# Splitting 64-bit weights: three vector passes a piece replaced by one rounding add into the low 16 bits

## The chip, the cores and the metric

The kernel runs on one core of one Trainium2 chip. The metric is the device time of one execution, in microseconds. Before the change the median of three runs is 871.97 us (870.41, 871.97 and 872.31).

## What is computed

A linear attention with a decaying state, then two blocks of dense layers. The activations are float32. The weights of both blocks are float64, since the setup divides them by a float64 square root. Cut to what matters:

```
state = 0                                   # per batch and head, 48 x 48
for t in range(768):
    y[t]  = r[t] @ (state + (u * k[t]) outer v[t])
    state = w * state + k[t] outer v[t]
x = y as 3072 tokens x 384
h = max(x @ w1, x @ w2, x @ w3)             # 384 -> 768, weights float64
x = h @ w_out                               # 768 -> 384
g, val = x @ w_gate, x @ w_val              # 384 -> 1536
out = (silu(g) * val) @ w_out2              # 1536 -> 384, float32
```

## The kernel before

**Products.** Every product of the dense layers runs on TensorE (PE) as three matmuls in the type float32r: high part of the weight by high part of the input (L429), high by low (L430), low by high (L431). So each weight is needed as two float32r tiles, its high and its low part. The tokens go in six blocks of 512 (index i). In the first block of layers a step f (of 6) makes three products `m` with 128 output channels each from the tile `w_a` of that step; the products `o` then use `w_b`; the second block of layers has products `g` and `oo` with `w_c`. The attention runs in 24 units n (six blocks of time, four batches): `s` (scores), `y` and `u` on PE. Unit n belongs to token block n // 4, so the units of block i + 1 are worked on between the products of block i.

**Pieces of weights.** A weight tile comes from DRAM in pieces k of 576 columns (384 for `w_b`), 42 in all: 12 for `w_a`, 6 for `w_b`, 24 for `w_c`. Pieces 0 to 14 are wanted while the first token block is worked on. A piece of 128 x 576 float64 lands as pairs of 32-bit words in the tile `raw` (three buffers); `lw` is the low and `hw` the high word, each read with a step of 8 bytes. `t` (two buffers) takes the float32 that is made of it. The steps of one piece in the kernel before:

- `fetch` (L212): the DMA from DRAM, in SP's queue.
- `scale` (L224), ScalarE (ACT): `hw`, read as float32, times 2^-112 into `t`.
- `top` (L257, L259), VectorE (DVE): shift and mask, then the sign put back: `t` is the weight cut off to a short mantissa.
- `rest` (L265, L267), DVE: the bits that were cut off, gathered from both words into `lw`.
- `power` (L272), DVE: the exponent bits of `t` into `hw`.
- `put_hi` (L275), ACT: `t` to the high part. `to_float` (L279), ACT: the integer in `lw` to float32.
- `put_lo` (L283), POOL: `hw` times `lw` to the low part.

**Order.** The order of the steps on each engine is not that of the code. `Plan.run` (L107) goes through a list of steps with needs and assumed costs and puts the step that can start first, weighted by the work behind it, next on its engine; engines then run their rows in that order. PE's order is written out by hand (L626 to L648). The steps of the pieces are added in L682 to L706; the numbers there (TOP, REST, POWER) are the planner's costs in us. A `fetch` of piece k needs `lo` of piece k - 3 (its buffer of `raw`), `scale` needs `hi` and `power` of piece k - 2 (its buffer of `t`). SP's queue is in order: a DMA whose buffer isn't free holds all behind it.

**The branch.** Some 33 us into the program all engines pass a branch (L615) that chooses between two forms of the recurrence. `fetch` of pieces 3 and on stands behind it, pieces 0 to 2 are loaded at the start. After it the first token block is split into a high part (`xhi`, L420, ACT) and a low part (`xlo`, L424, POOL: input less high part), as is every later one. For token block 1 and on, `repack` (L409, DMA) and `choose` (L415, DVE) come ahead of that.

Of the kernel before, what the change touches and what calls it, by code (L numbers as in the profile page):

```python
# [8 lines left out]
F32 = mybir.dt.float32  # L9
F32R = mybir.dt.float32r  # L10
U8 = mybir.dt.uint8
U32 = mybir.dt.uint32
I32 = mybir.dt.int32
AF = mybir.ActivationFunctionType
ALU = mybir.AluOpType
# [11 lines left out]
HALF = 576  # L27
# [60 lines left out]
class Plan:  # L88
# [8 lines left out]

    SHARED = ("top", "rest", "power", "lo", "xlo", "ylo", "scaled", "bonus", "choose")

# [73 lines left out]
def rwkv_moe(ctx: ExitStack, tc: tile.TileContext, qk, nat, kn, vn, rn, wcol, wh, uh, wup1, wout1, wup2, out):  # L173
# [80 lines left out]
    def top(k):  # L254

        t, hw = ts[k], words(k)[1]
        nc.vector.tensor_scalar(out=t, in0=t, scalar1=3, scalar2=0xFFFFF000,  # L257
                                op0=ALU.logical_shift_left, op1=ALU.bitwise_and)
        nc.vector.scalar_tensor_tensor(out=t, in0=hw, scalar=0x80000000, in1=t,  # L259
                                       op0=ALU.bitwise_and, op1=ALU.bitwise_or)  # L260

    def rest(k):

        lw, hw = words(k)
        nc.vector.tensor_scalar(out=hw, in0=hw, scalar1=0x1FF, scalar2=15,  # L265
                                op0=ALU.bitwise_and, op1=ALU.logical_shift_left)
        nc.vector.scalar_tensor_tensor(out=lw, in0=lw, scalar=17, in1=hw,  # L267
                                       op0=ALU.logical_shift_right, op1=ALU.bitwise_or)

    def power(k):  # L270

        nc.vector.tensor_scalar(out=words(k)[1], in0=ts[k], scalar1=0xFF800000, scalar2=None, op0=ALU.bitwise_and)  # L272

    def put_hi(k):
        nc.scalar.copy(part(k, 0), ts[k].bitcast(F32))  # L275

    def to_float(k):
        lw = words(k)[0]
        nc.scalar.mul(lw.bitcast(F32), lw, 2.0**-35)  # L279

    def put_lo(k, eng):
        lw, hw = (x.bitcast(F32) for x in words(k))
        eng.tensor_tensor(out=part(k, 1), in0=hw, in1=lw, op=ALU.mult)  # L283
        del raws[k], ts[k]

# [220 lines left out]
    with tc.manual_schedule():  # L506
# [175 lines left out]
        for k, (key, z, n, _) in enumerate(jobs):  # L682
            early = key[0] == "c" and key[1] < ASIDE
            own, pace, space = {}, [], []
            TOP, REST, POWER, share = (1.22, 1.22, 0.46, n / HALF) if key[0] != "c" else (1.22, 1.22, 0.46, 1.0) if early else (1.25, 1.25, 0.46, 1.0)
            if early:
# [4 lines left out]
            if k < 3:  # L691
                add(("fetch", k), {"none": 0.0}, [], lambda e: None, at=17.5 + 1.7 * k)
            else:
                add(("fetch", k), {"sync": 0.5}, [("lo", k - 3), ("branch",)] + pace, lambda e, k=k: fetch(k), lag=3.5, **own)
            cast = {"act": 0.2 + 0.48 * share}
            add(("scale", k), cast, [("fetch", k)] + ([("hi", k - 2), ("power", k - 2)] if k > 1 else []), lambda e, k=k: scale(k), **own)
            add(("top", k), {"dve": TOP * share}, [("scale", k)] + ([("power", k - 1)] if k else []), lambda e, k=k: top(k), **own)
            add(("rest", k), {"dve": REST * share}, [("top", k)], lambda e, k=k: rest(k), **own)
            add(("power", k), {"dve": POWER * share}, [("rest", k)], lambda e, k=k: power(k), **own)
            add(("hi", k), cast, [("top", k), ("rest", k)] + space + ([("put", k - 1)] if early and k > nearly else []),  # L700
                lambda e, k=k: put_hi(k), **own)
            add(("float", k), cast, [("rest", k)], lambda e, k=k: to_float(k), **own)
            add(("lo", k), {"pool": 1.2 * share, "dve": 0.76 * share}, [("float", k), ("power", k), ("hi", k)],
                lambda e, k=k: put_lo(k, engine[e]), **own)
# [210 lines left out]
```

## Time and profile before

| | |
|---|---|
| runs | 870.41, 871.97, 872.31 us; median 871.97 us |
| profiled execution | span 868.4 us from the first to the last instruction; its device time is not shown beside it |
| busy, whole span | PE 849.5 us (98%), DVE 404.0 (47%), ACT 317.6 (37%), POOL 195.6 (23%) |
| mean granted clock of PE | 0.994 of full speed |
| DMA | 74.33 MB, 86 GB/s over the span |

The span is 3.6 us under the median of the runs. A share of busy time is a mean over the whole span. The stages differ much: the span's 40 slices show DVE at nine tenths in slices 3 to 5 (44 to 109 us) and at two tenths in the second half, while PE stands at nine tenths from there to the end. A row of a group of instructions gives its line, engine, operation, tiles (written <- read), shape, count, then busy us and mean ns of one, then the idle time of the engine just ahead of them and what ended it. The prediction goes by the rows in the section below.

### The profile page before, as it was taken

The numbers are of one execution on the slowest core, as the hardware profiler recorded it, in microseconds if no ns is written. First come the engines' busy times: TensorE is split into PE (matmuls) and PEld (weight loads), VectorE is DVE, ScalarE is ACT, GpSimd is POOL, SyncE is SP. The second block draws the span as 40 slices with busy tenths as digits, with TensorE's granted clock in tenths as the row PEclk, the third lists the DMA queues.
The fourth block names the chain that finished last, engine by engine and source line by source line (L and its number), as shares of the span: only waits on it lengthen the run. The fifth ranks groups of instructions, "written<-read, shape, count | busy, mean of one in ns | idle before, by whom it ended". The sixth has DMA issues, their size and how long they took to land.

```text
span 868.4 us, 11958 instructions
## 1 busy us (share of the span) xinstructions
PE 849.5 (98%) x4794; PEld 697.5 (80%) x4794; DVE 404.0 (47%) x629; ACT 317.6 (37%) x634; POOL 195.6 (23%) x188
## 2 busy tenths in 40 slices
PE   9889799999999999999999999999999999999998
PEld 8667588888888888888888888888888888888886
DVE  4799977646746745313578422222222212122221
ACT  5666565344354443222455321131132122113111
POOL 7645453433523512100223300010010010001000
PEclk9899999999999999999999999999999999999999
DMA  8566424536346424421043100010000000001001
GB/s 286 194 204 204 162 85 121 164 126 196 137 138 188 159 84 160 173 105 59 11 127 109 37 1 1 0 37 1 1 37 1 1 1 36 1 1 37 0 1 37
DMA packets 21722, 74.33 MB, mean 86 GB/s; under 512 B 2496, under 2 KB 3392, under 8 KB 20896
## 3 DMA queue, kind: packets, MB, share of 16 engines
q1 hardware_dynamic: 21664, 73.54, 25.5%
q8 instruction: 38, 0.62, 0.3%
q14 instruction: 20, 0.16, 0.1%
HBM read 58.39 MB, written 14.16 MB: 84 GB/s over the span
## 4 chain that ended last, share of the span: by engine, by line
PE 87%; DVE 6%; issue 2%; ACT 0%; POOL 0%; ACTq 0%; DVEq 0%
PE g L429 11%; PE g L430 11%; PE g L431 11%; PE m L429 8%; PE m L430 7%; PE m L431 7%; PE oo L429 6%; PE oo L430 6%; PE oo L431 6%; PE o L431 3%; PE o L430 3%; PE o L429 3%; PE s L342 2%; PE y L371 2%; PE y L362 2%
## 5 line engine op out<-in xcount | busy, mean ns | idle before, releaser
L430 PE MATMUL g<-xlo,w_c 128*128 128x512 f32 x432 | 168.2, 389 | 0.0
L431 PE MATMUL g<-xhi,w_c 128*128 128x512 f32 x432 | 168.2, 389 | 0.0
L429 PE MATMUL g<-xhi,w_c 128*128 128x512 f32 x432 | 168.2, 389 | 0.0
L486 DVE TENSOR_TENSOR g<-mm,g 128x512 f32<-128x512 f32 x72 | 50.1, 696 | 243.5 <-PE g L431 243.4
L429 PE MATMUL m<-xhi,w_a 128*128 128x512 f32 x324 | 129.7, 400 | 1.6 <-ACT h L443 1.2
L431 PE MATMUL m<-xhi,w_a 128*128 128x512 f32 x324 | 127.0, 392 | 2.9 <-POOL w_a L283 2.9
L430 PE MATMUL m<-xlo,w_a 128*128 128x512 f32 x324 | 127.1, 392 | 1.6 <-POOL xlo L424 1.6
L482 ACT ACTIVATE mm<-g 128x512 f32<-128x512 f32 x72 | 43.0, 597 | 154.6 <-PE g L431 154.6
L424 POOL TENSOR_TENSOR xlo<-x,xhi 128x512 fp32r<-128x512 f32 x18 | 23.5, 1333 | 329.8 <-ACT xhi L420 329.8
L431 PEld LDWEIGHTS g<-xhi,w_c 128*128 128x128 f32 x432 | 81.1, 188 | 16.9
L429 PEld LDWEIGHTS g<-xhi,w_c 128*128 128x128 f32 x432 | 81.1, 188 | 16.8
L430 PEld LDWEIGHTS g<-xlo,w_c 128*128 128x128 f32 x432 | 81.1, 188 | 16.7
L491 ACT CAST gs<-g 128x512 fp32r<-128x512 f32 x72 | 42.2, 587 | 134.7 <-DVE g L486 134.7
L430 PE MATMUL oo<-gs,w_c 128*128 128x512 f32 x216 | 84.1, 389 | 0.0
L431 PE MATMUL oo<-gs,w_c 128*128 128x512 f32 x216 | 84.1, 389 | 0.0
L429 PE MATMUL oo<-gs,w_c 128*128 128x512 f32 x216 | 84.1, 389 | 0.0
L431 PEld LDWEIGHTS m<-xhi,w_a 128*128 128x128 f32 x324 | 60.9, 188 | 17.9 <-POOL w_a L283 5.2
L429 PEld LDWEIGHTS m<-xhi,w_a 128*128 128x128 f32 x324 | 60.8, 188 | 17.3 <-ACT h L443 1.5
L430 PEld LDWEIGHTS m<-xlo,w_a 128*128 128x128 f32 x324 | 60.9, 188 | 14.7 <-POOL xlo L424 3.0
L463 DVE TENSOR_TENSOR gs<-g,gs 128x512 fp32r<-128x512 f32 x72 | 49.8, 691 | 44.9 <-ACT gs L491 44.9
L333 ACT ACTIVATE am<-aeye,a 128x128 f32<-128x128 f32 x192 | 59.7, 392 | 23.2 <-DVE a L325 23.2
L460 ACT CAST hs<-m 128x512 fp32r<-128x512 f32 x33 | 19.3, 586 | 101.9 <-DVE m L448 101.4
(111 smaller groups left out, 1180.8 us busy)
## 6 DMA issues: line engine op xcount, KB each, us to landing
raw<-in_wup SPq DMA_DIRECT2D x36, 576.0 KB, 5.1
nat<-in_nat SPq DMA_DIRECT2D x22, 576.0 KB, 5.2
qk<-in_qk SPq DMA_DIRECT2D x24, 448.0 KB, 4.5
aside<-parts SPq DMA_DIRECT2D x12, 576.0 KB, 3.6
w_c<-aside SPq DMA_DIRECT2D x6, 1152.0 KB, 5.6
out<-ob SPq DMA_DIRECT2D x18, 256.0 KB, 2.1
y<-x SPq DMA_DIRECT2D x3, 768.0 KB, 10.7
raw<-in_wout SPq DMA_DIRECT2D x6, 384.0 KB, 3.3
```

The lines of the kernel that those rows point to most:

```text
L333: eng.mul(o, aeye, f)
L342: nc.tensor.matmul(sc[n][x][:, j], a[r:r + D, 1, j], a[r:r + D, 0, j], start=True, stop=True)
L362: nc.tensor.matmul(y[r:r + m, j], st[b][r:r + D, j * D:j * D + m], a[r:r + D, 0, j], start=j == 0, stop=False, skip_group_check=True)
L424: eng.tensor_tensor(out=lo[:, k], in0=t[:, k], in1=hi[:, k].bitcast(F32), op=ALU.subtract)
L429: nc.tensor.matmul(p, wh_, xh, start=first, stop=False)
L430: nc.tensor.matmul(p, wh_, xl, start=False, stop=False)
L431: nc.tensor.matmul(p, wl_, xh, start=False, stop=last)
L460: nc.scalar.copy(hsplit[i, f][0], banks["m", i, f, 2])
L463: nc.vector.tensor_tensor(out=g[1], in0=p, in1=g[0].bitcast(F32), op=ALU.subtract)
L482: nc.scalar.activation(out=hs[i, f], in_=banks["g", i, f, 0], func=AF.Silu)
L486: nc.vector.tensor_tensor(out=p, in0=hs[i, f], in1=p, op=ALU.mult)
L491: nc.scalar.copy(t[:, 0], banks["g", i, f, 1])
```

## The change

`top` keeps all bits that a float32 has room for: L257 loses its mask. `rest` becomes one pass (line 265 of the changed kernel): it views the low 16 bits of each word of `t` as uint16 and adds to them the low word of the weight times 2^-29, rounded by the write. So `t` is then the weight rounded to float32, and `raw` is free. `power` and `to_float` are gone. `put_hi` now comes behind `rest`; its cast to float32r rounds. `put_lo`, still on POOL, takes the high part off `t`. The needs follow: `fetch` of piece k waits for `rest` of k - 3 instead of `lo`, `scale` for `lo` of k - 2, since `t` is now read until the end. The planner's costs of `top` and `rest` change too.

```diff
     def top(k):
         t, hw = ts[k], words(k)[1]
-        nc.vector.tensor_scalar(out=t, in0=t, scalar1=3, scalar2=0xFFFFF000,
-                                op0=ALU.logical_shift_left, op1=ALU.bitwise_and)
+        nc.vector.tensor_scalar(out=t, in0=t, scalar1=3, scalar2=None, op0=ALU.logical_shift_left)
         nc.vector.scalar_tensor_tensor(out=t, in0=hw, scalar=0x80000000, in1=t,
                                        op0=ALU.bitwise_and, op1=ALU.bitwise_or)
     def rest(k):
-        lw, hw = words(k)
-        nc.vector.tensor_scalar(out=hw, in0=hw, scalar1=0x1FF, scalar2=15,
-                                op0=ALU.bitwise_and, op1=ALU.logical_shift_left)
-        nc.vector.scalar_tensor_tensor(out=lw, in0=lw, scalar=17, in1=hw,
-                                       op0=ALU.logical_shift_right, op1=ALU.bitwise_or)
-    def power(k):
-        nc.vector.tensor_scalar(out=words(k)[1], in0=ts[k], scalar1=0xFF800000, scalar2=None, op0=ALU.bitwise_and)
+        low = ts[k].bitcast(U16).rearrange("p (n z) -> p n z", z=2)[:, :, 0]
+        nc.vector.scalar_tensor_tensor(out=low, in0=words(k)[0], scalar=2.0**-29, in1=low,
+                                       op0=ALU.mult, op1=ALU.add)
+        del raws[k]
-    def to_float(k):
-        lw = words(k)[0]
-        nc.scalar.mul(lw.bitcast(F32), lw, 2.0**-35)
     def put_lo(k, eng):
-        lw, hw = (x.bitcast(F32) for x in words(k))
-        eng.tensor_tensor(out=part(k, 1), in0=hw, in1=lw, op=ALU.mult)
-        del raws[k], ts[k]
+        eng.tensor_tensor(out=part(k, 1), in0=ts[k].bitcast(F32), in1=part(k, 0).bitcast(F32), op=ALU.subtract)
+        del ts[k]
...
-            TOP, REST, POWER, share = (1.22, 1.22, 0.46, n / HALF) if key[0] != "c" else (1.22, 1.22, 0.46, 1.0) if early else (1.25, 1.25, 0.46, 1.0)
+            TOP, REST, share = (1.22, 0.76, n / HALF) if key[0] != "c" else (1.25, 0.8, 1.0)
...
-                add(("fetch", k), {"sync": 0.5}, [("lo", k - 3), ("branch",)] + pace, lambda e, k=k: fetch(k), lag=3.5, **own)
+                add(("fetch", k), {"sync": 0.5}, [("rest", k - 3), ("branch",)] + pace, lambda e, k=k: fetch(k), lag=3.5, **own)
-            add(("scale", k), cast, [("fetch", k)] + ([("hi", k - 2), ("power", k - 2)] if k > 1 else []), lambda e, k=k: scale(k), **own)
-            add(("top", k), {"dve": TOP * share}, [("scale", k)] + ([("power", k - 1)] if k else []), lambda e, k=k: top(k), **own)
+            add(("scale", k), cast, [("fetch", k)] + ([("lo", k - 2)] if k > 1 else []), lambda e, k=k: scale(k), **own)
+            add(("top", k), {"dve": TOP * share}, [("scale", k)] + ([("rest", k - 1)] if k else []), lambda e, k=k: top(k), **own)
-            add(("lo", k), {"pool": 1.2 * share, "dve": 0.76 * share}, [("float", k), ("power", k), ("hi", k)],
+            add(("lo", k), {"pool": 1.2 * share, "dve": 0.76 * share}, [("hi", k)],
```

PE has the same rows in the same order in both programs, tile for tile. The other engines' orders move, since the planner sees other costs and needs. In the rows below a number in a tile's name is the piece (`t_2`), the unit (`qk_4`) or the block and step (`m_0_1_2`); the last number only tells buffers apart.

VectorE from the branch on, before (in the change the lines behind `put_lo` are numbered 10 lower: L301 there is L311 here, L438 is L448):

```order
L265 TENSOR_SCALAR raw_1_131<-raw_1_131 128x576
L267 SCALAR_TENSOR_TENSOR raw_1_131<-raw_1_131 128x576
L272 TENSOR_SCALAR raw_1_131<-t_1_400 128x576
L257 TENSOR_SCALAR t_2_624<-t_2_624 128x576
L259 SCALAR_TENSOR_TENSOR t_2_624<-raw_2_133,t_2_624 128x576
L265 TENSOR_SCALAR raw_2_133<-raw_2_133 128x576
L267 SCALAR_TENSOR_TENSOR raw_2_133<-raw_2_133 128x576
L272 TENSOR_SCALAR raw_2_133<-t_2_624 128x576
L257 TENSOR_SCALAR t_3_642<-t_3_642 128x576
L259 SCALAR_TENSOR_TENSOR t_3_642<-raw_3_617,t_3_642 128x576
```

The same place on VectorE in the change:

```order
L258 TENSOR_SCALAR t_2_622<-t_2_622 128x576
L259 SCALAR_TENSOR_TENSOR t_2_622<-raw_2_133,t_2_622 128x576
L265 SCALAR_TENSOR_TENSOR t_2_622<-raw_2_133,t_2_622 128x576
L258 TENSOR_SCALAR t_3_639<-t_3_639 128x576
L259 SCALAR_TENSOR_TENSOR t_3_639<-raw_3_612,t_3_639 128x576
L438 TENSOR_TENSOR h_0_0_650<-h_0_0_650,m_0_0_1_667 128x512
L265 SCALAR_TENSOR_TENSOR t_3_639<-raw_3_612,t_3_639 128x576
L258 TENSOR_SCALAR t_4_700<-t_4_700 128x576
L259 SCALAR_TENSOR_TENSOR t_4_700<-raw_4_616,t_4_700 128x576
L301 TENSOR_TENSOR qk_4_662<-qk_4_662,powers_624 112x512 x2
```

Piece 1 is now done on VectorE ahead of the branch, and `top` of piece 4 stands ahead of the two passes on `qk_4`, which the first scores behind the branch (`s` of unit 4) wait for; before it stood behind them.

SP's queue from the branch on, before:

```order
L215 DMA raw_3_617<-in_wup1 128x1152
L304 DMA qk_4_665<-in_qk 112x1024
L305 DMA nat_4_666<-in_nat 128x1152
L215 DMA raw_4_683<-in_wup1 128x1152
L304 DMA qk_5_691<-in_qk 112x1024
```

The same place in SP's queue in the change:

```order
L216 DMA raw_3_612<-in_wup1 128x1152
L216 DMA raw_4_616<-in_wup1 128x1152
L294 DMA qk_4_662<-in_qk 112x1024
L295 DMA nat_4_663<-in_nat 128x1152
L216 DMA raw_5_683<-in_wup1 128x1152
```

Piece 4 moved ahead of the loads of unit 4.

VectorE at the end of the first token block (`choose` is L415, in the change L405), before:

```order
L257 TENSOR_SCALAR t_14_1269<-t_14_1269 128x384
L259 SCALAR_TENSOR_TENSOR t_14_1269<-raw_14_1227,t_14_1269 128x384
L265 TENSOR_SCALAR raw_14_1227<-raw_14_1227 128x384
L267 SCALAR_TENSOR_TENSOR raw_14_1227<-raw_14_1227 128x384
L272 TENSOR_SCALAR raw_14_1227<-t_14_1269 128x384
L404 TENSOR_TENSOR st_3_140<-st_3_140,u_7_1243 112x192
L448 TENSOR_TENSOR h_0_5_1229<-h_0_5_1229,m_0_5_1_1255 128x512
L448 TENSOR_TENSOR m_0_5_2_1276<-h_0_5_1229,m_0_5_2_1276 128x512
L311 TENSOR_TENSOR qk_8_1133<-qk_8_1133,powers_627 112x512
L415 COPY_PREDICATED xr_1_885<-slow_162,x2_1_89 128x1536
```

The same place on VectorE in the change:

```order
L258 TENSOR_SCALAR t_14_1233<-t_14_1233 128x384
L259 SCALAR_TENSOR_TENSOR t_14_1233<-raw_14_1168,t_14_1233 128x384
L265 SCALAR_TENSOR_TENSOR t_14_1233<-raw_14_1168,t_14_1233 128x384
L438 TENSOR_TENSOR h_0_5_1195<-h_0_5_1195,m_0_5_1_1210 128x512
L438 TENSOR_TENSOR m_0_5_2_1235<-h_0_5_1195,m_0_5_2_1235 128x512
L301 TENSOR_TENSOR qk_8_1120<-qk_8_1120,powers_624 112x512
L405 COPY_PREDICATED xr_1_872<-slow_162,x2_1_89 128x1536
```

`choose` of block 1 keeps its place behind piece 14, the last two maxima of block 0 and half of `qk_8`; two passes of piece 14 ahead of it are gone.

## Rows read from the trace of the kernel before

**Rows 1.** The page: the chain that ended last, shares of the span by engine.

```profile
PE 87%; DVE 6%; issue 2%; ACT 0%; POOL 0%; ACTq 0%; DVEq 0%
```

**Rows 2.** Stages: from:to, length, busy (count) of PE PEld DVE ACT POOL, clock, DMA, GB/s.

```profile
0.00:34.40 34.40, 30.84 (x274) 26.77 (x274) 19.09 (x46) 19.35 (x46) 24.13 (x35) 0.90 0.76 253
34.40:106.00 71.60, 60.54 (x493) 45.56 (x491) 68.58 (x108) 45.07 (x95) 36.63 (x34) 1.00 0.58 185
106.00:112.20 6.20, 6.20 (x20) 4.97 (x21) 5.62 (x8) 3.83 (x9) 6.09 (x5) 0.72 0.40 142
112.20:500.00 387.80, 387.80 (x2406) 319.00 (x2405) 223.98 (x344) 166.77 (x345) 113.60 (x105) 1.00 0.37 122
500.00:863.80 363.80, 363.80 (x1607) 301.24 (x1605) 86.43 (x125) 81.97 (x140) 15.13 (x12) 1.00 0.03 9
```

**Rows 3.** PE's waits from 34.4 to 106: total us, times, longest.

```profile
PE m L431 <- POOL w_a L283: 2.9, 4, 1.2
PE o L431 <- POOL w_b L283: 2.8, 2, 1.4
PE m L430 <- POOL xlo L424: 1.6, 3, 0.8
PE s L342 <- DVE qk L311: 1.6, 1, 1.6
PE m L429 <- ACT h L443: 1.2, 1, 1.2
PE u L390 <- DVE st L404: 0.6, 1, 0.6
PE m L429 <- ACT w_a L275: 0.3, 1, 0.3
```

**Rows 4.** Groups on VectorE from 34.4 to 106, shapes apart.

```profile
L267 DVE SCALAR_TENSOR_TENSOR raw<-raw 128x576 uint32<-128x576 uint32 x11 | 11.1, 1013 | 0.4
...
L265 DVE TENSOR_SCALAR raw<-raw 128x576 uint32<-128x576 uint32 x10 | 7.0, 705 | 0.1
L272 DVE TENSOR_SCALAR raw<-t 128x576 uint32<-128x576 uint32 x11 | 6.1, 558 | 0.3
...
L265 DVE TENSOR_SCALAR raw<-raw 128x384 uint32<-128x384 uint32 x3 | 1.7, 569 | 0.2
...
L272 DVE TENSOR_SCALAR raw<-t 128x384 uint32<-128x384 uint32 x3 | 1.1, 359 | 0.1
```

**Rows 5.** The timeline of VectorE from 37 us: start, us, instruction.

```profile
37.24 1.49 DVE L257 TENSOR_SCALAR t<-t 128x576 uint32<-128x576 uint32 x1 [1.22 <-ACT t L224]
38.77 1.58 DVE L259 SCALAR_TENSOR_TENSOR t<-raw,t 128x576 uint32<-128x576 uint32 x1
...
40.89 0.76 DVE L267 SCALAR_TENSOR_TENSOR raw<-raw 128x576 uint32<-128x576 uint32 x1
...
42.06 0.46 DVE L257 TENSOR_SCALAR t<-t 128x576 uint32<-128x576 uint32 x1
```

**Rows 6.** The timeline of POOL: while VectorE did the above, and two passes much later.

```profile
35.66 2.75 POOL L424 TENSOR_TENSOR xlo<-xr,xhi 128x512 fp32r<-128x512 f32 x2
...
484.49 1.15 POOL L283 TENSOR_TENSOR w_c<-raw 128x576 fp32r<-128x576 f32 x1 [3.70 <-ACT raw L279]
491.56 3.79 POOL L424 TENSOR_TENSOR xlo<-x,xhi 128x512 fp32r<-128x512 f32 x3 [5.92 <-ACT xhi L420]
```

**Rows 7.** The waits of the pieces from 34 to 112 (all engines; SP's queue).

```profile
ACT t L224 <- DMA raw<-in_wup: 9.2, 3, 5.1
...
SPq L215 <- POOL w_a L283: 36.2, 10, 7.2
```

**Rows 8.** The timeline of SP and ACT: the fetch of piece 4 and its `scale`.

```profile
40.28 0.39 SPq L215 DMA_DIRECT2D raw<-in_wup  x1
...
47.53 0.73 ACT L224 ACTIVATE t<-raw 128x576 f32<-128x576 f32 x1 [5.09 <-DMA raw<-in_wup]
```

**Rows 9.** The stage ahead of the low clock, columns as in rows 2.

```profile
88.00:106.00 18.00, 12.49 (x87) 8.60 (x85) 17.31 (x30) 10.02 (x21) 7.86 (x9) 1.00 0.40 131
```

More of the change, by code (lines that the diff above doesn't have):

```diff
@@ L11 @@
 U8 = mybir.dt.uint8
+U16 = mybir.dt.uint16
 U32 = mybir.dt.uint32
@@ L95, in __init__ @@
         self.behind = {}
-    SHARED = ("top", "rest", "power", "lo", "xlo", "ylo", "scaled", "bonus", "choose")
+    SHARED = ("top", "rest", "lo", "xlo", "ylo", "scaled", "bonus", "choose")
     def add(self, key, on, needs, do, lag=0.0, at=0.0, behind=None):
@@ L693, in rwkv_moe @@
             else:
-                add(("fetch", k), {"sync": 0.5}, [("lo", k - 3), ("branch",)] + pace, lambda e, k=k: fetch(k), lag=3.5, **own)
+                add(("fetch", k), {"sync": 0.5}, [("rest", k - 3), ("branch",)] + pace, lambda e, k=k: fetch(k), lag=3.5, **own)
             cast = {"act": 0.2 + 0.48 * share}
-            add(("scale", k), cast, [("fetch", k)] + ([("hi", k - 2), ("power", k - 2)] if k > 1 else []), lambda e, k=k: scale(k), **own)
-            add(("top", k), {"dve": TOP * share}, [("scale", k)] + ([("power", k - 1)] if k else []), lambda e, k=k: top(k), **own)
+            add(("scale", k), cast, [("fetch", k)] + ([("lo", k - 2)] if k > 1 else []), lambda e, k=k: scale(k), **own)
+            add(("top", k), {"dve": TOP * share}, [("scale", k)] + ([("rest", k - 1)] if k else []), lambda e, k=k: top(k), **own)
             add(("rest", k), {"dve": REST * share}, [("top", k)], lambda e, k=k: rest(k), **own)
-            add(("power", k), {"dve": POWER * share}, [("rest", k)], lambda e, k=k: power(k), **own)
-            add(("hi", k), cast, [("top", k), ("rest", k)] + space + ([("put", k - 1)] if early and k > nearly else []),
+            add(("hi", k), cast, [("rest", k)] + space + ([("put", k - 1)] if early and k > nearly else []),
                 lambda e, k=k: put_hi(k), **own)
-            add(("float", k), cast, [("rest", k)], lambda e, k=k: to_float(k), **own)
-            add(("lo", k), {"pool": 1.2 * share, "dve": 0.76 * share}, [("float", k), ("power", k), ("hi", k)],
+            add(("lo", k), {"pool": 1.2 * share, "dve": 0.76 * share}, [("hi", k)],
                 lambda e, k=k: put_lo(k, engine[e]), **own)
```

## The prediction

> **What bounds the kernel now.** The chain that ended last is 87% PE and 6% DVE [rows 1]. Such a share is a mean, so I cut the span into stages [rows 2]: the reader is to look for a stage in which PE isn't busy throughout. From 112.2 to 863.8 us PE is busy for 387.80 of 387.80 and 363.80 of 363.80 us: there nothing that another engine saves can shorten anything. Ahead of 34.4 us TensorE waits for the attention's first units, and only pieces 0 and 1 are worked on. One stage is left: from 34.4 to 106 PE is busy for 60.54 of 71.60 us, so it stands still for 11.1 us, while DVE is busy for 68.58 us, 96%. So in this stage VectorE is the bound, and it's the stage in which pieces 2 to 14 have to be there in time. Behind it, from 106.0 to 112.2, the granted clock is 0.72, a mixture of 2.4 and 1.2 GHz, after a stretch (88 to 106 us) in which PE was busy for only 12.49 of 18 us [rows 9]. That costs 6.20 x 0.28 = 1.7 us more. What the change can reach at most is thus 11.1 + 1.7 = 12.8 us of 868.4.
>
> Next, what PE waits for there [rows 3]. Three kinds, told apart by who is late:
> - weights: 2.9 and 2.8 us for the low part (POOL L283), 0.3 for the high part: 6.0 us;
> - VectorE's queue: 1.6 for `qk` of unit 4, 1.2 for a copy on ACT that stands behind a maximum on DVE, 0.6 for the state: 3.4 us;
> - the first `xlo` behind the branch: 1.6 us.
>
> **The change, part by part.** VectorE first. Per piece L265 and L272 go. In the stage that is 7.0 + 6.1 us for the wide pieces and 1.7 + 1.1 for the narrow ones, 15.9 us [rows 4]. All groups on VectorE in this stage add up to 74.5 us where the engine is busy for 68.58, since neighbouring rows overlap a little; so the removed ones are worth 15.9 x 68.58 / 74.5 = 14.6 us of its time. L257 loses only its mask: a pass with one operand over 576 words takes 0.46 us alone [rows 5], and the same with one operation instead of two; nothing. The new L265 takes the place of L267, with the same number of elements and two sources. No row shows a pass that writes 16-bit words with a step of 4 bytes and mixes types. Nearest is L267 itself, 0.76 us alone [rows 5] and 1.01 in the stage [rows 4]; a gain below that is excluded, since two sources at 576 elements never ran faster here; the other end is taken as twice, 1.5 us. I take 0.76. So VectorE's load falls from 68.6 to 54.0 us, where PE's own work is 60.5: the bound goes to PE, with VectorE close behind, at nine tenths.
>
> ACT loses `to_float` (L279), 42 passes. ACT is busy for 45.07 of 71.60 us [rows 2], so its load counts for nothing; what counts is that a piece goes through one pass less before POOL.
>
> POOL: `put_lo` now reads two tiles, `t` and the high part, instead of two halves of one. Alone it took 1.15 us for 576 elements, while the like subtraction `xlo` takes 3.79 / 3 = 1.26 us for 512 [rows 6], which makes 1.42 for 576. I take 1.42, bounds 1.15 and 1.5: 0.27 more a piece. POOL is busy for 36.63 of 71.60 us, so this is covered unless VectorE has to wait for it (a rival below).
>
> The fetches: the longest of SP's waits in this stage is the one of `fetch` for `put_lo` of the piece three earlier, 36.2 us in ten waits [rows 7]; it now waits for `rest`, two steps earlier. Piece 4 gains most: before, its DMA stood behind the load of unit 4, was issued at 40.28, and ACT waited for it for 5.09 us until 47.53 [rows 8]; now it is issued right behind piece 3, with which the queue goes on after the branch at some 33 us: 7 us earlier. The loads of unit 4 that it's moved past come later by one issue, 0.4 us [rows 8], and on VectorE `qk_4` stands behind three pieces in any case. In turn `scale` waits for `put_lo` of the piece two earlier: with two buffers of `t` a piece may take two times 5 us from `scale` to the end (a step of PE, some 10 us, uses two pieces), and needs about 0.73 + 0.46 + 0.76 + 0.76 + 0.73 + 1.42 = 4.9 without waits (the high part's cast on ACT taken like `scale` [rows 8]). It fits, and I cost it at nothing; should VectorE lag, it is the first thing to be late.
>
> What is late next: the split of token block 1. PE goes from the last `y` of block 0 through `u`, two products `m` (18 matmuls) and 27 of `o` without a gap, some 11 us; `repack`, `choose` and the split need nearly as long, and before were hidden behind late weights. I count 0.5 us of new waits there.
>
> The sum. Weight waits 6.0 to 1.0: -5.0. VectorE's queue 3.4 to 1.4, since it stays at nine tenths: -2.0. `xlo` stays. New wait: +0.5. The low clock: with PE busy for more than nine tenths of the stretch ahead of it, as it is behind 112 us where the clock is 1.00, I take -1.4 of 1.7. Sum: -7.9 us. The span would be 868.4 - 7.9 = 860.5. The profiled execution's span stands 3.6 us under the median of the runs; with that the time is **864.1 us**.
>
> **The rivals.**
>
> *All of it.* VectorE is no bound at all, and every wait for weights and for its queue goes with the low clock: 6.0 + 3.4 + 1.7 = 11.1, so 860.9 us. For it: 14.6 us less load. Against: the rows keep their order, and nine tenths of a strict order leave waits. Chance 0.23.
>
> *VectorE stays the bound.* The two passes that stay have two sources each, and rows show what POOL does to them: while it ran `xlo` from 35.66 on, L257 took 1.49 instead of 0.46 and L259 1.58 instead of 0.76 [rows 5, 6]. If VectorE waits for the longer `put_lo` each time, 14 x 0.27 = 3.8 us come back: -4.1, 867.9 us. The same end is reached if the 16-bit pass takes 1.5 us: 14 x 0.76 x 0.92 = 9.8 of the 14.6 us come back, VectorE's load is 63.8, above PE's 60.5, and 4.8 us remain, 867.2. Chance 0.22. The Trainium skill has the rule to this ("SBUF — State Buffer", section Who interferes with whom): a VectorE instruction with two SBUF inputs and a GpSimd instruction that reads SBUF shut each other out for the whole instruction. By that rule each longer `put_lo` is paid in full whenever VectorE stands at a two-source pass, which speaks against this change; the trace agrees as far as the two stretched rows go. On the price the skill differs from my row ("GPSIMD Engine Reference", section 3.1): about 2.6 cycles at 1.2 GHz per element of a two-input pass, an estimate of 1.25 us for 576 whatever the tiles; by it this rival would cost 1.4 instead of 3.8 us. The rows (1.15 and 1.26 x 576 / 512) don't bear out one price for both, so the sum goes by them.
>
> *Slower: the 16-bit pass is dear.* If a half word is written by reading the whole word first, or the change of types takes several turns, the pass can cost more than what it saves. It decides from 15.9 / 14 = 1.14 us above L267's 0.76, at 1.9 us. At four times L267, 3.0 us, 14 x 2.28 - 15.9 = 16 us more load, 14.7 of VectorE's time, all on the bound: 886.7 us. Nothing in the profile has such a row, nor one near it. Chance 0.05.
>
> *Input-bound.* The pieces wait for their DMA instead: ACT did so for 9.2 us in three waits [rows 7]. If each comes through to PE, only the 2.0 of VectorE's queue are won: 870.0. Against: the DMA engines are busy for 58% of the stage [rows 2], and fetches start earlier. Chance 0.05.
>
> That the change doesn't take its steps out can be excluded: VectorE has two rows fewer a piece and ACT one.
>
> **The numbers.** Forecast, 864.1 us and 2 us to either side: 0.45. The range takes in all of it (860.9) and the case with VectorE as the bound (867.9), with 1 us on either side for the runs, which lie 1.9 us apart: 859.5 to 869.0; outside are the dear pass, the input and the edges, less than 0.2. No change means within 0.2%, 1.7 us, about what a measurement of this kernel can tell. Faster, below 870.2: the first three cases and part of the fourth, 0.89. Same: 0.05. Slower: 0.06.
>
> **What would show it.** Right: no DVE rows of two extra passes a piece; the new pass at 0.76 us alone; PE's idle time between the branch and token block 1 down from 11 to 4 or 5 us, DVE at nine tenths there; no low clock around 100 us; `put_lo` at about 1.4 us alone; PE busy throughout from some 102 us on, the same 752 us to its end. Wrong: the pass above 1.5 us, waits of PE for `w_a` or `w_b` as long as before, a wait of several us for `xhi` or `xlo` of block 1, or PE waits behind 112 us, where there were none.

## The result and the profile after

The changed kernel takes 862.83 us in the median of four runs (861.79 to 865.69), the kernel before 871.41 us on the same chip (870.41 to 872.31). The ratio is 0.9909, with a 95% interval of 0.9889 to 0.9929: 8.6 us off, where the forecast was 7.9.

The profiled execution of the change, with a span of 864.0 us, is the slowest of its four (865.69 us), and its time is 1.7 us above its span. The profiled span of before, 868.4 us, is 3.6 us below its median. So the two profiles lie nearer to each other (4.4 us) than the medians do, and the rows below understate the gain.

The page of the change, its busy times and its chain:

```profile
PE 847.5 (98%) x4794; PEld 697.1 (81%) x4794; DVE 362.9 (42%) x545; ACT 292.7 (34%) x592; POOL 210.7 (24%) x188
...
PE 88%; DMA 3%; POOL 3%; DVE 2%; issue 2%; ACT 1%; SPq 1%; POOLq 0%; ACTq 0%; DVEq 0%
```

VectorE has 84 rows fewer (629 to 545) and ScalarE 42 (634 to 592). VectorE's share of the chain fell from 6% [rows 1] to 2%; DMA and POOL have come in with 3% each.

The stages of the change, columns as in [rows 2] (from:to, length, busy of PE PEld DVE ACT POOL, clock, DMA, GB/s):

```profile
34.40:106.00 71.60, 66.20 (x526) 52.65 (x526) 59.37 (x86) 40.86 (x89) 45.74 (x36) 0.98 0.64 193
106.00:112.00 6.00, 4.50 (x28) 2.91 (x28) 2.08 (x4) 4.41 (x12) 5.92 (x6) 1.00 0.00 0
112.00:500.00 388.00, 388.00 (x2397) 319.35 (x2396) 197.55 (x292) 148.54 (x310) 119.61 (x101) 1.00 0.37 122
...
52.00:58.00 6.00, 4.58 (x13) 3.66 (x14) 4.63 (x8) 4.48 (x13) 0.97 (x1) 0.72 0.27 68
```

Between 34.4 and 106 us PE is now busy for 66.20 instead of 60.54 us, VectorE for 59.37 instead of 68.58, POOL for 45.74 instead of 36.63 [rows 2]. This fixed stretch doesn't hold the same work in both: the change gets further in it (526 of PE's matmuls instead of 493). From 112 to 500 us nothing is different: PE has no idle time. The low clock that stood at 106 us before is gone from there; this execution has one of the same depth (0.72) at 52 to 58 us.

PE's waits in the change, from 34.4 to 112 us (total us, times, longest), to be held against [rows 3]:

```profile
PE m L420 <- POOL xlo L414: 3.1, 6, 0.9
PE m L419 <- ACT h L433: 2.3, 1, 2.3
PE s L332 <- DVE qk L301: 0.6, 1, 0.6
PE o L419 <- ACT w_b L270: 0.5, 1, 0.5
PE o L421 <- POOL w_b L273: 0.4, 1, 0.4
```

The waits for `w_a` are gone altogether and those for `w_b` fell to 0.9 us: 6.0 us of weight waits have become 0.9. `xlo` has doubled, from three waits to six; the three new ones are those of token block 1. The wait for `h` has grown from 1.2 to 2.3.

One measure serves for all runs below: the time on PE from the start of the first product `m` behind the branch to the start of the first scores `s` of unit 8, which stand behind the first two products of token block 1. It doesn't depend on when the branch is reached. Before it is 34.41 to 114.19, 79.8 us; in the change (timeline of PE) 36.20 to 110.14, 73.9 us:

```profile
36.20 0.49 PE L419 MATMUL m<-xhi,w_a 128*128 128x512 f32 x1
...
53.42 0.53 PE L419 MATMUL m<-xhi,w_a 128*128 128x512 f32 x1 [2.25 <-ACT h L433]
...
110.14 1.16 PE L332 MATMUL s<-qk 48*128 48x128 f32 x16
```

Over this measure PE does the same rows in both (some 520 matmuls; before, then the change):

```profile
34.41:114.19 79.78, 68.72 (x520) 51.76 (x518) 74.19 (x115) 50.87 (x110) 44.71 (x39) 0.98 0.55 177
36.20:110.14 73.94, 67.04 (x521) 52.16 (x519) 60.41 (x87) 42.64 (x96) 49.88 (x39) 0.98 0.60 184
```

VectorE's busy time for this work fell from 74.19 to 60.41 us, by 13.8. Of PE's 5.8 us, 4.2 are idle time (11.1 to 6.9). The other 1.7 lie within PE's busy time (68.72 to 67.04); no row says in what. The change's execution reaches the branch later, which takes 1.8 us of it back in its span.

### The profile page after: what moved, and what is told of

It is laid out like the page before. It is cut to its first block, busy times and chain, and to the rows that moved or that the text cites. A ratio compares the mean times of both kernels' runs of the same rounds, so it can differ in the third digit from the quotient of the medians.

```text
span 864.0 us, 11768 instructions
## 1 busy us (share of the span) xinstructions
PE 847.5 (98%) x4794; PEld 697.1 (81%) x4794; DVE 362.9 (42%) x545; ACT 292.7 (34%) x592; POOL 210.7 (24%) x188
## 4 chain that ended last, share of the span: by engine, by line
PE 88%; DMA 3%; POOL 3%; DVE 2%; issue 2%; ACT 1%; SPq 1%; POOLq 0%; ACTq 0%; DVEq 0%
PE g L420 11%; PE g L421 11%; PE g L419 11%; PE m L419 8%; PE m L420 7%; PE m L421 7%; PE oo L420 6%; PE oo L421 6%; PE oo L419 6%; PE o L421 3%; PE o L419 3%; PE o L420 3%; PE s L332 2%; PE y L361 2%; PE y L352 2%
## 5 line engine op out<-in xcount | busy, mean ns | idle before, releaser
L335 DVE COPY_PREDICATED am<-mask,s 128x512 f32<-128x512 uint8 x48 | 33.4, 735 | 45.5 <-PE s L332 40.1
```

Of the source, the lines that this page charges most:

```text
L335: nc.vector.copy_predicated(ams[n][:, x], mask[:, None, :].to_broadcast([128, NPAIR, T]), sc[n][x])
```

## Experiments

Runs of one group below ran on the same chip and share the runs of the kernel before: e1 to e4 (its median 870.37 us), e5 to e8 (870.13), e9 to e11 (872.32), e12 (870.33).

### Where the two passes count: e1 and e2

The change, with two one-source passes back on VectorE behind the new one, into the dead tile `raw`: in e1 for the 15 pieces of the first token block, in e2 for the 27 others.

```diff
+        if k < 15:
+            lw, hw = words(k)
+            nc.vector.tensor_scalar(out=hw, in0=hw, scalar1=0x1FF, scalar2=15,
+                                    op0=ALU.bitwise_and, op1=ALU.logical_shift_left)
+            nc.vector.tensor_scalar(out=hw, in0=ts[k], scalar1=0xFF800000, scalar2=None, op0=ALU.bitwise_and)
```

In e2 the condition is `k >= 15`.

> The changed kernel, with two single-source passes on VectorE put behind the new pass of each of pieces 0 to 14 (same shapes as the two that the change removed; they write words of raw that nobody reads). The planner's costs are left as they are, so every engine keeps its order. Theory (VectorE's load in the first token block is what the change relieves): about 13 us of load are back in that stage, most of the gain is lost, 868 to 873 us, ratio to the kernel before 0.997 to 1.003, with PE waits for w_a and w_b back. Rival (the gain comes from earlier fetches and the shorter chain of a piece): at most 3 us are lost, 862 to 866.

> The same two passes, but behind pieces 15 to 41 only, 54 passes where the run on the first pieces has 30. Theory: behind 112 us PE is busy throughout and VectorE has room, so nothing is lost: 861.5 to 864.5 us, ratio to the kernel before 0.989 to 0.993. Rival (load on VectorE counts wherever it is): about twice the loss of the run with the passes in the first block.

Measured: e1 872.19 us, ratio to before 1.0021 (1.0012 to 1.0030); e2 862.47 us, ratio 0.9903 (0.9888 to 0.9919). Thirty passes in the first block take the whole gain back, 54 passes later take nothing. The window of e1 shows the bound of before again:

```profile
34.40:106.00 71.60, 60.81 (x488) 48.03 (x488) 69.29 (x106) 35.90 (x80) 38.37 (x32) 0.95 0.60 181
```

VectorE 69.29 and PE 60.81 us busy, next to 68.58 and 60.54 [rows 2]. One part of e1's theory missed: the weight waits didn't come back in full (2.2 us from 34.4 to 112 us, where the kernel before has 6.0 and the change 0.9); the largest wait of PE is 3.6 us for VectorE's `qk`. The kernel of e2 is that of the change up to piece 14, so its profile is a second look at the stage: 73.5 us from `m` to `s`, as in the change (73.9), with the clock at 1.00 throughout.

### Those two passes alone: e3

The kernel before, without L265 and L272; its own order and needs, the rest of the 8 steps kept. The low part is then not the weight's.

```diff
-        nc.vector.tensor_scalar(out=hw, in0=hw, scalar1=0x1FF, scalar2=15,
-                                op0=ALU.bitwise_and, op1=ALU.logical_shift_left)
...
-        nc.vector.tensor_scalar(out=words(k)[1], in0=ts[k], scalar1=0xFF800000, scalar2=None, op0=ALU.bitwise_and)
+        pass
```

> The kernel before, in its own order, with its needs, its fetch behind put_lo and its to_float on ACT, but the two single-source passes of each piece (L265 and L272) left out. So the low part is not that of the weight: the gathering of the cut-off bits and the exponent are not computed. Theory (VectorE's load): most of the gain is there without the rest of the change, 862 to 866 us, ratio 0.988 to 0.994. Rival (fetch order, buffers of raw, one pass less on ACT): no gain worth speaking of, 869 to 872.

Measured: 860.01 us, ratio 0.9881 (0.9865 to 0.9896), 69.6 us from `m` to `s`. Taking the two passes away gives more than the whole change does; e3 lies below the range that its theory gave, and the rest of the change costs 2.4 us by the ratios (0.0028 of 871), though the intervals touch. Its fetches still wait for `put_lo`, so the gain is there without the moved fetches. What costs these 2.4 us is the question of the remaining runs.

### Piece 4's fetch: e4

The change, with the fetch of piece 4 back behind the loads of unit 4 in SP's queue.

```diff
-[("rest", k - 3), ("branch",)] + pace
+[("rest", k - 3), ("branch",)] + ([("load", 4)] if k == 4 else []) + pace
```

> The changed kernel with one more need: the fetch of piece 4 stands behind the loads of unit 4 in SP's queue, as in the kernel before. Theory (VectorE's load): it costs at most 1.5 us, 861 to 865. Rival (the early fetch of piece 4 is a good part of the gain): 3 us or more lost, 866 and up. Third view: in the profiled run of the change ACT stood 4.7 us behind the DMA of piece 5 and PE then waited 2.3 us for a copy on ACT; if the early fetch of piece 4 crowds that DMA, this run is faster by 1 to 2 us, 860 to 862.

Measured: 863.76 us, ratio 0.9929 (0.9912 to 0.9946): 0.9 us above the change by the medians, 1.7 by the ratios, and the intervals overlap. PE's waits in its profile have one that the change doesn't have:

```profile
PE m L419 <- ACT w_a L270: 3.0, 1, 3.0
```

This execution also has a low clock around that wait (0.95 over the stage from 34.4 to 106 us, against 0.98 in the change's). So the moved fetch may be worth 1 to 2 us; that isn't settled.

### The new wait for `h`: e5

The longest wait in the change's profile, 2.25 us before the `m` at 53.42, has a plain chain behind it. ScalarE's timeline:

```profile
42.12 0.75 ACT L225 ACTIVATE t<-raw 128x576 f32<-128x576 f32 x1 [3.24 <-POOL w_a L273]
...
51.70 0.71 ACT L225 ACTIVATE t<-raw 128x576 f32<-128x576 f32 x1 [4.66 <-DMA raw<-in_wup]
52.32 0.57 ACT L450 CAST hs<-m 128x512 fp32r<-128x512 f32 x1
52.78 0.59 ACT L433 COPY h<-m 128x512 f32<-128x512 f32 x1
```

The `scale` of piece 5 waits 4.66 us for its DMA (issued at 42.84 us, while the DMA engines were busy for 0.92 of the time from 43 to 52 us), and the copy `h` that PE needs stands behind it in ScalarE's order. e5 tells the planner of a longer transfer, so that the copies come ahead of the `scale`; PE's order is the same.

```diff
-lambda e, k=k: fetch(k), lag=3.5, **own)
+lambda e, k=k: fetch(k), lag=9.0 if k == 5 else 3.5, **own)
...
-lambda e, n=n: load_unit(n), lag=4.2)
+lambda e, n=n: load_unit(n), lag=10.0 if n == 5 else 4.2)
```

> The change, with the planner told that the fetch of piece 5 takes 9.0 us instead of 3.5 and the loads of unit 5 10.0 instead of 4.2. ScalarE's order then has the scale of piece 5 behind the copies hs of step 0, h of step 1 and the high-part cast of piece 4, instead of ahead of them; PE's order is the same. Theory (the new 2.25 us wait of PE for the copy h, and the low clock of 52 to 58 us behind it, come from the scale of piece 5 that holds ScalarE while its DMA is under way): that wait is gone, and the time is 1.5 to 4 us below the change's 862.8, so 859 to 861.3, ratio to the kernel before about 0.987 to 0.9895. Rival (piece 5 is late by itself, so the products of its step wait instead): a wait of 2 to 3 us for w_a stands in the place of the one for h, and the time stays within 1 us of the change's.

Measured: 861.93 us, ratio 0.9912 (0.9899 to 0.9924): nothing. The theory falls. One of PE's waits from 34.4 to 106 us shows why:

```profile
PE m L421 <- POOL w_a L273: 1.4, 3, 0.8
```

The wait for `h` is gone, and 1.4 us for `w_a` stand in its place: the chain of pieces itself is late, and PE meets it one way or the other. That is the rival's pattern, with half of its size.

### The split of token block 1: e6 and e7

In the change `xlo` of block 1 is late on POOL (timeline):

```profile
101.09 2.52 POOL L387 TENSOR_TENSOR st<-st,pw 112x192 f32<-112x192 f32 x1
103.58 1.01 POOL L305 TENSOR_TENSOR nat<-nat 128x384 f32<-128x384 f32 x1
104.67 1.03 POOL L306 TENSOR_TENSOR nat<-nat,ub 128x384 f32<-128x384 f32 x1
105.64 3.78 POOL L414 TENSOR_TENSOR xlo<-xr,xhi 128x512 fp32r<-128x512 f32 x3
```

It stands behind the state and two passes on the next unit, and begins without a wait of its own: its input was there. e6 puts it on VectorE; e7 is e5 and e6 together.

```diff
-add(("xlo", i, k), both, [("xhi", i, k)], lambda e, i=i, k=k: split_lo((1, i), xr[i], k, engine[e]))
+add(("xlo", i, k), {"dve": 0.65} if i == 1 else both, [("xhi", i, k)], lambda e, i=i, k=k: split_lo((1, i), xr[i], k, engine[e]))
```

> The change, with the low part of token block 1 (xlo) split off on VectorE instead of POOL, where it stood behind passes over unit 8. Theory (the three waits of PE for it, 0.94 + 0.28 + 0.27 us, come from POOL's queue and from POOL's slower pass): they fall to 0.3 us or less in sum, 1 to 1.5 us off, 861.3 to 861.8, ratio about 0.9895 to 0.990. Rival (the split's input, made by repack and choose, is what comes late): the same waits stand there, with VectorE as what is waited for, and the time stays within 0.5 us of the change's 862.8.

> Both edits of the two runs above in one kernel. If the two waits are separate, as the theory has it, their gains add up: 2.5 to 5.5 us below the change, 857.3 to 860.3, ratio about 0.985 to 0.9885, and the kernel beats both the one before and the change. Rival (block 1 begins by something else, such as VectorE's maxima, whatever was won ahead of it): no more than the larger one of the two alone.

Measured: e6 860.29 us, ratio 0.9889 (0.9869 to 0.9909), its runs from 857.87 to 864.25; e7 860.43 us, 0.9888 (0.9874 to 0.9902). In e6 PE has no wait left for `xlo` of block 1. Its 1.7 us (0.0020 of 871) are a little more than the theory gave, but its interval overlaps the change's, so they aren't settled. The two edits together are worth what e6 is alone, as the rival of e7 has it, which bears out that e5 was worth nothing.

### The length of `put_lo`: e8, e10 and e11

Three kernels replace `put_lo` alone, with every row in the place it has in the change. The prediction had costed its new length at nothing, outside the rival in which VectorE waits for it.

```diff
-eng.tensor_tensor(out=part(k, 1), in0=ts[k].bitcast(F32), in1=part(k, 0).bitcast(F32), op=ALU.subtract)
+eng.tensor_copy(part(k, 1), ts[k].bitcast(F32))
```

This is e8. The added line in e10, and then in e11:

```diff
+eng.tensor_copy(part(k, 1), part(k, 0).bitcast(F32))
...
+eng.tensor_tensor(out=part(k, 1), in0=ts[k].bitcast(F32), in1=ts[k].bitcast(F32), op=ALU.subtract)
```

> The change, with put_lo on POOL as a copy of t into the low part's tile instead of t less the high part: one source, the same rows in the same order. The low part of the weights is left out of the computation (the tile holds the rounded weight). Theory (the longer put_lo, 1.42 us alone and 1.55 to 1.68 in the mean, costs the change little, since POOL has time; where it holds t and stretches VectorE it costs at most 1 us): the pass falls to 0.6 to 1.2 us and the time to 861.8 to 862.8. Rival (put_lo's length and its reads beside VectorE's are what keeps the change 2.4 us behind the kernel before with two passes left out): 860 to 861, with VectorE's new pass shorter in the stage from 34 to 106 us than 1.22 us in the mean.

> The change, with put_lo on POOL as a copy of the high part into the low part's tile: one source as in the run with t copied, but behind put_hi again, as in the change; t is free from put_hi on. The rows are in the order of the change. The low part of the weights is left out of the computation. Theory A (holding of t): 856.5 to 859, since t is free even before put_lo. Theory B (length and sources of put_lo): 856.5 to 859 as well. Theory C (the wait for put_hi): 861 to 863, as the change.

> The change, with put_lo on POOL as t less t: two sources and a length as in the change (1.2 to 1.45 us alone), but no wait for put_hi, as in the run with t copied; t is held until its end. The rows are in the order of the change. The low part of the weights is left out of the computation (it is zero). Theory B (length and sources): 861 to 863, as the change. Theory C (the wait for put_hi): 856.5 to 858.5, as the run with t copied. Theory A (holding of t): between, 858.5 to 861, since t is held for one pass of ScalarE less, some 0.7 us a piece, of the change's 1.55 + 0.7.

Measured: e8 856.83 us, ratio 0.9851 (0.9838 to 0.9864); e10 857.71 us, 0.9846 (0.9825 to 0.9867); e11 860.64 us, 0.9873 (0.9850 to 0.9896). In e8 the theory that gave `put_lo` 1 us at most falls, and its rival gave too little as well: 5 us hang on it, and the intervals of e8 and e10 lie clear of the change's. e11 lies in the range that the holding of `t` (theory A) gave for it. The groups on POOL from 34.4 to 106 us, first the change, then e8, e10 and e11:

```profile
L273 POOL TENSOR_TENSOR w_a<-t,w_a 128x576 fp32r<-128x576 f32 x11 | 17.0, 1547 | 16.1 <-ACT w_a L270 16.1
...
L273 POOL TENSOR_TENSOR w_b<-t,w_b 128x384 fp32r<-128x384 f32 x3 | 3.4, 1149 | 4.6 <-ACT w_b L270 4.6
```

```profile
L273 POOL CAST w_a<-t 128x576 fp32r<-128x576 f32 x11 | 8.4, 763 | 14.2 <-DVE t L265 14.2
...
L273 POOL CAST w_b<-t 128x384 fp32r<-128x384 f32 x3 | 1.7, 552 | 4.5 <-DVE t L265 4.5
```

```profile
L273 POOL CAST w_a<-w_a 128x576 fp32r<-128x576 f32 x11 | 8.7, 794 | 18.7 <-ACT w_a L270 18.7
```

```profile
L273 POOL TENSOR_TENSOR w_a<-t 128x576 fp32r<-128x576 f32 x11 | 13.6, 1236 | 17.7 <-DVE t L265 17.7
...
L273 POOL TENSOR_TENSOR w_b<-t 128x384 fp32r<-128x384 f32 x3 | 2.5, 835 | 4.5 <-DVE t L265 4.5
```

The wait for `put_hi` on ScalarE isn't the cause: e10 has it, as the change, e8 and e11 don't, and the short pass gives the same time with that wait as without it. From the change to e8 the passes lose 20.4 - 10.1 = 10.3 us, and the time falls by 0.0058 x 871 = 5.1 us: half a microsecond for each. From the change to e11 it is 20.4 - 16.1 = 4.3 us for 3.1, a share that isn't settled, since the intervals meet.

A shorter pass acts in two ways at once, and these runs don't part them: it holds `t` for less time, so that the `scale` two pieces later starts earlier, and it stands less in VectorE's way. In the change `scale` waits for the wide pieces' `put_lo` five times between 34.4 and 106 us, a wait that the kernel before doesn't have:

```profile
ACT t L225 <- POOL w_a L273: 5.7, 5, 3.2
```

It is 2.5 us in e8, 3.0 in e11 and nothing in e10. VectorE's busy time from `m` to `s`, 60.41 us in the change, is 56.52 in e8 and 55.73 in e10, but 61.94 in e11: there `put_lo` starts right behind L265 and meets the next piece's L259, which takes 1.27 us in the mean instead of 0.92. So by these profiles what e11 gains on the change isn't VectorE's time.

In e8 PE has next to no wait but `xlo` from the first `m` to the first `s` of unit 8, which takes 101.17 - 33.34 = 67.8 us (the window, then the waits):

```profile
33.34:101.17 67.83, 64.79 (x520) 51.18 (x518) 56.52 (x87) 42.69 (x96) 36.36 (x39) 1.00 0.64 201
```

```profile
PE m L420 <- POOL xlo L414: 2.9, 6, 0.8
PE s L332 <- DVE qk L301: 0.2, 1, 0.2
```

How a pass on POOL comes to cost VectorE shows in the two timelines of the change, side by side. VectorE:

```profile
39.09 1.72 DVE L259 SCALAR_TENSOR_TENSOR t<-raw,t 128x576 uint32<-128x576 uint32 x1
40.85 1.93 DVE L265 SCALAR_TENSOR_TENSOR t<-raw,t 128x576 uint16<-128x576 uint32 x1
...
45.01 1.32 DVE L265 SCALAR_TENSOR_TENSOR t<-raw,t 128x576 uint16<-128x576 uint32 x1
...
434.94 0.82 DVE L265 SCALAR_TENSOR_TENSOR t<-raw,t 128x576 uint16<-128x576 uint32 x1
...
459.46 1.95 DVE L265 SCALAR_TENSOR_TENSOR t<-raw,t 128x576 uint16<-128x576 uint32 x1
```

POOL:

```profile
40.17 1.92 POOL L273 TENSOR_TENSOR w_a<-t,w_a 128x576 fp32r<-128x576 f32 x1
44.21 1.43 POOL L273 TENSOR_TENSOR w_a<-t,w_a 128x576 fp32r<-128x576 f32 x1 [2.13 <-ACT w_a L270]
...
449.92 1.42 POOL L273 TENSOR_TENSOR w_c<-t,w_c 128x576 fp32r<-128x576 f32 x1 [2.27 <-ACT w_c L270]
...
458.78 1.94 POOL L273 TENSOR_TENSOR w_c<-t,w_c 128x576 fp32r<-128x576 f32 x1 [2.03 <-ACT w_c L270]
```

These are three of the five times in this execution that a wide L265 meets a `put_lo` that is under way. It ends 0.69 us behind POOL's end (42.78 and 42.09, 46.33 and 45.64, 461.41 and 460.72), however long it had been there before; in the other two, at 32.94 and 63.34 us, it is 0.66 and 0.67. Alone it takes 0.82. So next to nothing of it runs beside `put_lo`: a two-source pass on VectorE pays what is left of POOL's pass. POOL pays in turn: the `put_lo` that starts at 40.17 us, while L259 is under way, ends 1.28 us behind L259's end at 40.81, and takes 1.92 instead of 1.42. The one-source copy does the same in e8, only shorter; VectorE and POOL there:

```profile
37.99 1.19 DVE L265 SCALAR_TENSOR_TENSOR t<-raw,t 128x576 uint16<-128x576 uint32 x1
```

```profile
37.29 1.19 POOL L273 CAST w_a<-t 128x576 fp32r<-128x576 f32 x1
```

L265 ends at 39.18, 0.70 us behind the copy's end at 38.48. So in such a meeting it is the length of POOL's pass that counts, not its number of sources.

### A third buffer of `t`, alone and with the edit of e6: e9 and e12

`put_lo` also holds `t`, and with two buffers the `scale` two pieces later waits for it: 3.24 us at 42.12 in ScalarE's timeline above. e9 gives pieces 2 to 17 a third buffer, the order being that of the change. e12 adds the edit of e6 to it.

```diff
-ts[k] = raw_p.tile([128, HALF], U32, tag="t", name=f"t_{k}")[:, 0:jobs[k][2]]
+aside_t = k % 3 == 2 and k < nearly
+ts[k] = (xpool.tile([128, HALF], U32, tag=f"x2_{NB - 1}", name=f"t_{k}") if aside_t
+         else raw_p.tile([128, HALF], U32, tag="t", name=f"t_{k}"))[:, 0:jobs[k][2]]
```

> The change with a third buffer of t for pieces 2 to 17 (pieces 2, 5, 8, 11, 14 and 17 get it, in space that nothing else uses by then); every engine's rows are in the order of the change, and nothing else is different. Theory A (what costs the change its 6 us against the run with the low part copied is that put_lo holds a buffer of t until its end, so the scale of the piece two later starts late): 857 to 859.5, ratio to the kernel before 0.985 to 0.988, and ScalarE's waits of scale for POOL's w_a in the first block are gone. Theory B (it is the length of put_lo and its two sources beside VectorE's): 861.8 to 863, as the change. Theory C (it is the low part's wait for ScalarE's put_hi ahead of it): as B.

> The change with both edits that took something off: the third buffer of t (the run of it alone had the ratio 0.9879 to the kernel before), and the low part of token block 1 split off on VectorE (0.9889 alone). Theory (they remove different waits: scale for POOL in the first block, and PE for xlo at the start of block 1): the ratio is 0.985 to 0.987, and from PE's first product to its first scores of block 1 it takes 68.5 to 69.5 us, against 73.9 in the change's profile. Rival (they free the same engine, POOL, and so overlap): no better than the third buffer alone, 0.9875 to 0.989 and 70 to 71 us. Either way put_lo keeps its length, so the 67.8 us of the runs with a short put_lo aren't reached.

Measured: e9 860.97 us, ratio 0.9879 (0.9855 to 0.9904), 70.2 us from `m` to `s`; e12 858.73 us, ratio 0.9865 (0.9849 to 0.9882), 69.4 us. In e9 no `scale` waits for POOL in the first block any more, but the time lies between what theory A and theory B gave, and its interval meets the change's: the holding of `t` is a part, 2.6 us by the ratios, about half of what e8 gives, and isn't settled by itself. e12 lies clear of the change, within what its theory gave, and is the best kernel here that computes both parts of every weight. Its window and waits (lines are two higher in this kernel):

```profile
34.40:106.00 71.60, 67.84 (x541) 53.28 (x542) 62.19 (x90) 41.67 (x95) 48.48 (x38) 1.00 0.61 190
```

```profile
PE m L422 <- POOL xlo L416: 1.6, 3, 0.8
PE m L423 <- POOL w_a L275: 0.8, 2, 0.4
PE m L421 <- ACT h L435: 0.6, 1, 0.6
PE o L423 <- POOL w_b L275: 0.4, 1, 0.4
```

PE is busy for 67.84 us of the stage, 1.6 more than in the change. What is left of `xlo` is the first one behind the branch, as before the change.

## Why the prediction was right

**The bound: right.** VectorE was the bound in the first token block and nowhere else. e1 and e2 show it directly: the same two passes are worth everything there and nothing later.

**VectorE's load: right, but not by the terms that it was made of.** The sum took 14.6 us off. Over the same rows of PE, from `m` to `s`, VectorE's busy time fell by 13.8. (The 9.2 us between the two fixed stages say less, since in the change `choose` and more passes on later units fall into the stage.) The term that was mis-sized is the price of the new L265: the sum set it equal to L267, since 0.76 was taken for both alone. Alone it is 0.82 us, near that. In the stage it isn't alone:

```profile
L265 DVE SCALAR_TENSOR_TENSOR t<-raw,t 128x576 uint16<-128x576 uint32 x11 | 13.5, 1223 | 0.2
L259 DVE SCALAR_TENSOR_TENSOR t<-raw,t 128x576 uint32<-128x576 uint32 x10 | 9.2, 924 | 0.3
...
L265 DVE SCALAR_TENSOR_TENSOR t<-raw,t 128x384 uint16<-128x384 uint32 x3 | 3.2, 1061 | 0.1
```

L267, which it replaces, had a mean of 1013 ns here [rows 4], and the new pass has 1223. Of the 14 passes in these two rows six met a `put_lo` under way and four a pass of POOL over the attention units; the four others took their time alone. With the narrow pieces L265 is 3.9 us above L267 in the stage. That the load still fell nearly as forecast is luck in part: L257 and L259, which the sum left as they were, took 1.9 us less together.

**`put_lo`: the length right, its cost wrong.** It is 1.42 us alone, as worked out from `xlo`. But "covered unless VectorE has to wait for it" was the wrong side of that condition. In the stage it went from 17.5 us (14.6 for the wide pieces and 2.9 for the narrow ones) to 20.4; at the half microsecond a microsecond that e8 shows, these 2.9 us cost some 1.5. This is an estimate, and it leaves out that `put_lo` held no `t` before; e3, with 16.0 us of `put_lo` and without that hold, is 2.4 us ahead. The second rival had named this mechanism and charged the longer part in full, 3.8 us: that VectorE waits for `put_lo` is shown, and by this estimate about half of each microsecond is paid. One of the two rows on which the rival rested was misread: `xlo` ended at 38.41 us [rows 6], before L259 began at 38.77 [rows 5]; what L259 met is the `put_lo` that POOL's timeline of before has from 38.38 to 39.74, and it ended 0.61 us behind it. The other, L257, has one source and isn't a case of a two-source pass. The rule of the Trainium skill ("SBUF — State Buffer", section Who interferes with whom), that a VectorE instruction with two SBUF inputs and a GpSimd instruction that reads SBUF shut each other out for the whole instruction, agrees with the 0.66 to 0.69 us by which L265 ended behind POOL each time.

**The hold of `t`: costed at nothing, and it is late.** The prediction had 4.9 us of a piece's steps fit into two times 5 us, and called it the first thing to be late should VectorE lag. VectorE is less busy than before (60.41 of 73.94 us from `m` to `s`, after 74.19 of 79.78), and it is late all the same: `scale` waits 5.7 us for the wide pieces' `put_lo`, and 3.24 of them at 42.12 us, since that `put_lo` stood behind `xlo` (on POOL from 36.23 to 40.20 us) and then waited for L259. For the same reason piece 4 gains less than the 7 us that the prediction gave it: its `scale` waits for `put_lo` now, not for the DMA, and starts at 45.67 instead of 47.53 us. e9, which takes the hold away, is 2.6 us ahead of the change, not settled.

**The waits.** Weights: forecast 6.0 to 1.0, measured 0.9. VectorE's queue: forecast 3.4 to 1.4, measured 2.9 in this profile (0.6 for `qk`, 2.3 for `h`); the 2.3 come from the late DMA of piece 5, not from VectorE, and e5 shows that `h` is only where PE meets the late chain of pieces, not a cause. `xlo` behind the branch: 1.6, as forecast. Split of token block 1: forecast 0.5, measured 1.5, and not from `repack` and `choose`, as the prediction had it, but from POOL's queue; e6 removes it. The low clock at 106 us went, as forecast (-1.4); but one of the same size stands at 52 to 58 us in this execution, behind the 2.25 us in which PE stood still, so in this profile the term gave nothing. In the profiles of e2, e3 and e5 to e12 the mean clock of the stage is 1.00, in those of e1 and e4 0.95.

**The sum.** By these rows, with nothing for the clock, it is -5.1 - 0.5 + 1.5 = -4.1 us instead of -7.9, and PE's idle time did fall by 4.2 between the two profiles. The medians differ by 8.6. What is missing lies in two places. The runs here take 1.7 us more than their span, so the profiled execution of before took some 870.1 us and was 1.3 below the median of 871.41, while that of the change was 2.9 above its own, 1.8 of them by its later start. And 1.7 us are in PE's busy time, where no row tells what they are. So the forecast was right in place, sign and size, but not term by term: less came from VectorE's queue and more was lost at block 1 than it had, and that the sum still agrees with the medians is in part luck. The number alone doesn't part it from the first rival either (860.9, all of it): the measured 862.83 lies between the two. The waits do: `h`, `qk` and `xlo` are still there.

**The moved fetch**, which the prediction let gain time for piece 4 and costed at nothing for the loads it passes: undoing it gains nothing, and costs 1 to 2 us if anything (e4). **The dear 16-bit pass** is excluded: 0.82 us alone. **Input-bound**: one wait of this kind is left in the stage, the 4.66 us for piece 5, where 9.2 us stood before [rows 7]; PE met it as the 2.25 us for `h`.

## What to carry to other kernels

A pass that is taken off the engine that bounds a stage is worth its time in that stage only; look for the stage first, and put the same passes back elsewhere to prove it. Measure the effect over the same work (here from `m` to `s`), not over the same microseconds, or later work that moved in hides part of it. Price what is added by its time in the stage, beside the work that it will meet, not by the row in which it ran alone: here a two-source pass on VectorE waited out POOL's pass, and a step that holds a buffer made the next piece late, so a longer step on a POOL with idle time wasn't free. And where one late chain feeds several waits, moving the wait (e5) gains nothing; shortening the chain does (e8), and so does a buffer that lets it start earlier together with a shorter queue on POOL (e12).

## What the runs showed of the hardware

- The new pass, which reads 32-bit words with a step of 8 bytes, reads and writes 16-bit words with a step of 4 and converts between them, takes 0.82 us for 576 elements, nearly as little as the two-source pass on whole words (0.76).
- POOL takes 1.42 us for the difference of two tiles of 576 elements, but 1.15 for the difference of a tile to itself (e11, at 440.15 us of its span) and for the product of two halves of one tile [rows 6], and 0.67 for a copy (e8):

```profile
440.15 1.15 POOL L273 TENSOR_TENSOR w_c<-t 128x576 fp32r<-128x576 f32 x1 [3.60 <-DVE t L265]
```

```profile
448.72 0.67 POOL L273 CAST w_c<-t 128x576 fp32r<-128x576 f32 x1 [2.69 <-DVE t L265]
```

- A one-source copy on POOL shuts a two-source pass on VectorE out as a two-source one does (0.70 us behind its end in e8 and 0.67 to 0.69 in the three wide meetings of e10, against 0.66 to 0.69 in the change).
